# A fused speech-joint forward and backward kernel: pinning the gelu derivative's operations on DVE to their place in the source

## The chip, the cores and the metric

The kernel runs on one core of a Trainium2 chip. The metric is the device time of one execution in microseconds (us). Engines are named as in the profile: PE (TensorE), DVE (VectorE), ACT (ScalarE), POOL (GpSimd) and SP (the queue that issues most loads).

## The reference

The function is a small network and all its gradients. `x` is (2, 16000, 256), `g` is (2, 8, 256), all in bfloat16.

```
h = gelu(conv3(x, w1))[:, ::2]          # 2 x 8000 x 256
f = gelu(conv3(h, w2))[:, ::2]          # 2 x 4000 x 256
fe = f @ w_f;  ge = g @ w_g
j  = tanh(fe[:, :, None] + ge[:, None]) # 2 x 4000 x 8 x 256
out = j @ w_o
# returned: out, and the vjp of grad_out for x, w1, w2, g, w_f, w_g, w_o
```

Backward needs the derivative of both gelus. The gelu is the tanh form, computed as x * sigmoid(A x (1 + K x^2)).

## The kernel before

**Chunks.** Each batch entry has 4000 output rows, cut into 8 chunks: seven of 512 and one of 416, so 16 chunks `n`. For one chunk the forward part is the first convolution (L247, even and odd output rows, `par` 0 and 1), its gelu into `HT`, the second convolution (L280), its gelu into `FT`, and `FE` (L303, L305). The joint part runs over 8 values of `u`, two at a time (`up` 0 to 3): tanh into `JT` (L313), its square `JSQ` (L537), the gradient's product with `w_o` (L543), which DVE turns into `NGZ` (L545, two instructions for each `u`), a running sum of `NGZ` on POOL (L564, tile `ACCN`, the last one `NGFE`), the output matmuls (L641) and their eviction `OUT` (L643, ACT), and the weight gradient `GWO_ps` (L690). In chunk 0 the transposed `JT` that L690 needs is made on PE (L393) and copied by DVE (L395, tile `JR`); in the others a DMA makes it.

**What runs beside what.** `weave` takes the joint units of chunk n as the main line and puts between them, by a ratio, filling units: the forward part of chunk n+1 and the backward part of chunk n-1, which is `GF` (L349, L351, from `NGFE` and `G2`), `GH` (L379, L382, from `GF` and `G1`), the weight gradients (L419, L451, L515, summed on DVE at L332) and the input gradient (L492, evicted by ACT at L495). Chunk 0's forward part runs ahead of the loop, in a prologue.

**The gelu's operations.** `gelu()` issues nothing; it returns two lists. `first` (two on ACT, two on DVE) gives the gelu itself and goes into the queue `later`. `second` gives the derivative (`G1` for the first convolution, `G2` for the second): five DVE operations for each gelu of a chunk, two tensor-scalar and three tensor-tensor operations of 128x1024 bfloat16, and for chunk 0 ten of 128x512. They go into the queue `lazy`, with two small POOL copies of `G1`'s edge column (L259, L263). After each unit of the main line `pump` issues one operation (two while `later` holds some): those of `later` first (their records carry L198), then those of `lazy` (records L200), and these only after `lazy_on` was set at the end of the second convolution:

```
def weave(main, fill, ratio):
    due = 0.0
    for _ in main:
        pump(2 if later else 1)
```

What is left of `lazy` is issued at the end of the chunk. So in the source a chunk's fifteen derivative operations stand behind the second convolution of the same chunk, spread over the units of the last joint pairs.

**What sets the order.** The order on each engine isn't that of the source. The tile framework's scheduler reorders what is independent, and put the derivative operations where their operands are ready, which is earlier than the source has them. An instruction given to `tc.keep_in_program_order` is queued behind the instruction that was traced before it on its engine; it is an order of issue and adds no wait for another engine. Before, only the prologue's warm-up matmuls and the loads `X5` on POOL's queue are pinned.

**Buffers.** The PSUM pool `psp` has 7 banks, shared by all tiles `ps` and `pst`; a matmul that takes a bank waits until the engine that evicts its last content has read it. `JSQ` has 2 buffers, so the square for `u` waits until both `NGZ` of `u-2` are done; `NGZ` has 3 (POOL frees them); the gelu's scratch `g_sq` and `g_s` 3 each; `G1` and `G2` 2.

Of the kernel before, what the change touches and what calls it, by code (L numbers as in the profile page):

```python
# [33 lines left out]
def kernel(  # L34
# [157 lines left out]
    later, lazy = deque(), deque()  # L192
    lazy_on = [False]

    def pump(k):
        for _ in range(k):
            if later:
                later.popleft()()  # L198
            elif lazy and lazy_on[0]:
                lazy.popleft()()  # L200

    def gelu(xb, W, h, gp, off, kts=((0, KT),), spare=False):

# [24 lines left out]
    def conv_units(n):  # L228
# [11 lines left out]
        for par in range(2):  # L240
            xb = gel.tile([P, KT, CW], BF16, name="g_x")
            for mt in range(KT):
                ps = ps_f32()
                k = 0
                for (i, c, sh) in taps[par]:
                    for kt in range(KT):
                        nc.tensor.matmul(ps[:, :W], lhsT=W1[:, i, kt, mt * P:(mt + 1) * P],  # L247
                                         rhs=st["X", c][:, kt, 16 + sh:16 + sh + W], start=(k == 0), stop=(k == 5))
                        k += 1
                nc.scalar.copy(out=xb[:, mt, :W], in_=ps[:, :W])  # L250
                yield
            first, second = gelu(xb, W, HT[:, par], G1[:, par], 2, HALVES if n == 0 else ((0, KT),), n == 0)
            later.extend(first)
            seconds += second
            if n == 0:
                pump(len(first))
# [8 lines left out]
    def conv2_units(n):  # L265
        b, ci, c0, W = geom(n)
        st = S[n]
        HT = st["HT"]
        if n > 0:
            pump(len(later))  # L270
        FT = ftp.tile([P, KT, CW], BF16, name="FT")
        G2 = ftp.tile([P, KT, CW], BF16, name="G2")
        st["FT"], st["G2"] = FT, G2
        xb = gel.tile([P, KT, CW], BF16, name="g_x")
        for mt in range(KT):
            ps = ps_f32()
            k = 0
            for (i, par, off) in ((1, 0, 2), (0, 1, 1), (2, 1, 2)):
                for kt in range(KT):
                    nc.tensor.matmul(ps[:, :W], lhsT=W2[:, i, kt, mt * P:(mt + 1) * P],  # L280
                                     rhs=HT[:, par, kt, off:off + W], start=(k == 0), stop=(k == 5))
                    k += 1
            nc.scalar.copy(out=xb[:, mt, :W], in_=ps[:, :W])
            yield
        first, second = gelu(xb, W, FT, G2, 0, HALVES if n == 0 else ((0, KT),), n == 0)
        if n == 0:
            for f in first:
                f()
        else:
            later.extend(first)  # L290
        lazy.extend(second)
        lazy_on[0] = True

    def fe_units(n):
        b, ci, c0, W = geom(n)
        if n > 0:
            pump(len(later))
        FE = fep.tile([P, KT, CW], FP32, name="FE")
        S[n]["FE"] = FE
        for mt in range(KT):  # L300
            ps = ps_f32()
            for kt in range(KT):
                nc.tensor.matmul(ps[:, :W], lhsT=WF[:, kt, mt * P:(mt + 1) * P], rhs=S[n]["FT"][:, kt, :W],  # L303
                                 start=(kt == 0), stop=(kt == KT - 1))
            nc.scalar.copy(out=FE[:, mt, :W], in_=ps[:, :W])  # L305
            yield
# [595 lines left out]
```

## Time and profile before

| what | value |
|---|---|
| three runs | 857.64, 857.89, 858.03 us; median 857.89 |
| the profiled execution | 858.94 us, its span 857.2 us, so 1.74 us lie outside the span |
| busy in the span | PE 824.1 us (96%), ACT 671.8 (78%), DVE 583.3 (68%), POOL 406.4 (47%) |
| granted TensorE clock | 0.997 of full speed on average |
| L200 records | 15 chunks of 128x1024 or 128x832 operations in 42.1 to 778 us, thirty of 128x512 in 12.9 to 30.5 us |
| the stages | prologue and chunk 0 up to 72.7 us, then about 51.9 us for a full chunk (127.7 to 179.6 us is one) |

A chunk is counted here from the first `GF` eviction (L351) to the next. The chunks are alike from the third on, except where a batch entry ends (384 to 433 us, and the end), so that two stretches stand for all: the first 73 us, and one full chunk.

### The profile page before, as it was taken

The numbers are of one execution on the slowest core, as the hardware profiler recorded it, in microseconds if no ns is written. First come the engines' busy times: TensorE is split into PE (matmuls) and PEld (weight loads), VectorE is DVE, ScalarE is ACT, GpSimd is POOL, SyncE is SP. The second block draws the span as 40 slices with busy tenths as digits, with TensorE's granted clock in tenths as the row PEclk, the third lists the DMA queues.
The fourth block names the chain that finished last, engine by engine and source line by source line (L and its number), as shares of the span: only waits on it lengthen the run. The fifth ranks groups of instructions, "written<-read, shape, count | busy, mean of one in ns | idle before, by whom it ended". The sixth has DMA issues, their size and how long they took to land.

```text
span 857.2 us, 17222 instructions
## 1 busy us (share of the span) xinstructions
PE 824.1 (96%) x6478; PEld 598.7 (70%) x6552; DVE 583.3 (68%) x1190; ACT 671.8 (78%) x1064; POOL 406.4 (47%) x452
## 2 busy tenths in 40 slices
PE   8888999999999999999999999999999999999998
PEld 3455777767668677777767677776776767778876
DVE  4697858658585784859578495875858668495552
ACT  4788897886959869696996959879596886969533
POOL 1255554535535445554553555443553535545650
PEclk9999999999999999999999999999999999999999
DMA  9899999999999999979999999999999999998952
GB/s 189 186 202 219 207 219 221 233 210 216 271 224 226 220 210 267 243 201 231 201 184 215 238 216 238 202 240 257 225 265 210 259 229 191 216 213 199 215 161 90
DMA packets 379280, 185.60 MB, mean 217 GB/s; under 512 B 326786, under 2 KB 362907, under 8 KB 379198
## 3 DMA queue, kind: packets, MB, share of 16 engines
q1 hardware_dynamic: 359550, 115.19, 74.7%
q0 software_dynamic: 19648, 69.32, 26.9%
q8 instruction: 51, 0.84, 0.4%
q14 instruction: 31, 0.25, 0.1%
HBM read 54.43 MB, written 50.34 MB: 122 GB/s over the span
## 4 chain that ended last, share of the span: by engine, by line
ACT 33%; DVE 32%; PE 27%; issue 5%; DMA 2%; POOL 0%; ACTq 0%; DVEq 0%; POOLq 0%
DVE NGZ L545 10%; ACT JT L313 8%; ACT OUT L643 7%; DVE G L200 4%; DVE g_sq L200 4%; ACT JSQ L537 4%; ACT g_sq L198 4%; PE ps L543 4%; DVE GH L382 4%; DVE g_s L198 4%; ACT GX L495 3%; PE ps L515 3%; PE ps L492 3%; PE GWO_ps L690 3%; PE ps L641 3%
## 5 line engine op out<-in xcount | busy, mean ns | idle before, releaser
L564 POOL TENSOR_TENSOR ACCN<-ACCN,NGZ 128x1024 f32<-128x1024 f32 (+1 forms) x80 | 170.7, 2134 | 128.5 <-DVE NGZ L545 126.1
L537 ACT ACTIVATE JSQ<-JT 128x1024 bf16<-128x1024 bf16 (+1 forms) x128 | 133.9, 1049 | 112.4 <-DVE NGZ L545 112.4
L545 DVE SCALAR_TENSOR_TENSOR NGZ<-JSQ,ps 128x512 bf16<-128x512 bf16 (+1 forms) x256 | 163.1, 669 | 77.7 <-PE GWO_ps L690 37.7
L313 ACT ACTIVATE JT<-FE,GE 128x512 bf16<-128x512 f32 (+1 forms) x256 | 171.0, 728 | 0.5
L641 PE MATMUL ps<-WO,JT 128*128 128x256 bf16 x992 | 148.0, 272 | 1.6 <-DVE NGZ L545 0.5
L643 ACT CAST OUT<-ps 128x512 bf16<-128x512 f32 x248 | 145.9, 606 | 2.9 <-PE ps L641 2.8
L690 PE MATMUL GWO_ps<-GO,JR 128*128 128x256 bf16 x992 | 139.9, 273 | 0.0
L543 PE MATMUL ps<-GOT,WOT 128*128 128x512 bf16 (+1 forms) x472 | 134.5, 373 | 3.8 <-DVE JR L395 1.3
L641 PEld LDWEIGHTS <-JT 128*128 128x128 bf16 x992 | 95.5, 98 | 29.5 <-issue 2.2
L198 DVE SCALAR_TENSOR_TENSOR g_s<-g_sq,g_x 128x1024 bf16<-128x1024 bf16 (+1 forms) x45 | 55.9, 1242 | 83.5 <-ACT g_sq L198 83.5
L690 PEld LDWEIGHTS <-JR 128*128 128x128 bf16 x992 | 95.2, 98 | 18.0 <-issue 0.8
L492 PE MATMUL ps<-W1T,GH 128*128 128x256 bf16 (+2 forms) x768 | 104.2, 273 | 0.0
L670 POOL DMA_DIRECT2D out_dram<-OUT x64 | 49.4, 773 | 98.7 <-ACT OUT L643 97.4
L247 PE MATMUL ps<-XC,W 128*128 128x512 bf16 (+1 forms) x370 | 89.7, 377 | 3.3 <-DMA XC<-in_x_dram 2.7
L515 PE MATMUL ps<-rows,X 128*128 128x256 bf16 (+2 forms) x768 | 92.3, 273 | 0.0
L332 DVE TENSOR_TENSOR ACC<-ACC,ps 128x512 f32<-128x512 f32 x84 | 56.1, 682 | 41.5 <-PE ps L515 40.3
L495 ACT CAST GX<-ps 128x512 bf16<-128x512 f32 (+2 forms) x128 | 72.9, 594 | 14.3 <-PE ps L492 11.6
L492 PEld LDWEIGHTS <-GH 128*128 128x128 bf16 (+2 forms) x768 | 75.0, 99 | 12.4 <-issue 1.1
L515 PEld LDWEIGHTS <-X 128*128 128x128 bf16 (+2 forms) x768 | 74.6, 98 | 12.9 <-issue 1.3
L543 PEld LDWEIGHTS <-WOT 128*128 128x128 bf16 x512 | 48.5, 98 | 43.1 <-issue 2.0
L247 PEld LDWEIGHTS <-W 128*128 128x128 bf16 x384 | 37.7, 99 | 41.0 <-issue 4.7
L505 POOL DMA_DIRECT2D out_dram<-GX x60 | 33.7, 561 | 57.7 <-ACT GX L495 51.8
(139 smaller groups left out, 1282.0 us busy)
## 6 DMA issues: line engine op xcount, KB each, us to landing
GO<-in_grad_out_dram SPq DMA_DIRECT2D x56, 512.0 KB, 5.1
out_dram<-OUT POOLq DMA_DIRECT2D x56, 512.0 KB, 5.9
X<-in_x_dram POOLq DMA_DIRECT2D x58, 320.0 KB, 8.6
out_dram<-GX POOLq DMA_DIRECT2D x55, 256.0 KB, 4.2
GO<-in_grad_out_dram SPq DMA_DIRECT2D x8, 384.0 KB, 4.0
out_dram<-OUT POOLq DMA_DIRECT2D x8, 384.0 KB, 4.8
JR<-JT SPq DMA_TRANSPOSE x136, 5.3
GOT<-in_grad_out_dram SPq DMA_TRANSPOSE x128, 4.8
```

The costliest lines, as they stand in the source:

```text
L198: later.popleft()()
L247: nc.tensor.matmul(ps[:, :W], lhsT=W1[:, i, kt, mt * P:(mt + 1) * P], rhs=st["X", c][:, kt, 16 + sh:16 + sh + W], start=(k == 0), stop=(k ...
L313: nc.scalar.activation(out=JT[:, mt, :W], in_=S[n]["FE"][:, mt, :W], func=ACT.Tanh, bias=GE[:, b, mt, u:u + 1], scale=1.0)
L492: nc.tensor.matmul(ps[:Mx, cj * D:(cj + 1) * D], lhsT=GH[:, par, kt, j:j + Mx], rhs=W1T[:, i, kt, :], start=(k == 0), stop=(k == last))
L515: nc.tensor.matmul(ps[:, dt * D:(dt + 1) * D], lhsT=st["X5", o][:M, i + 2 * par, dt * P:(dt + 1) * P], rhs=t[:M, j + 2 * par:j + 2 * par + ...
L537: nc.scalar.activation(out=JSQ[:, :, :W], in_=JT[:, :, :W], func=ACT.Square)
L543: nc.tensor.matmul(ps[:, :W], lhsT=WOT[:, kt, mt * P:(mt + 1) * P], rhs=GOT[:, kt, :W], start=(kt == 0), stop=(kt == KT - 1))
L545: nc.vector.scalar_tensor_tensor(out=NGZ[:, mt, :W], in0=JSQ[:, mt, :W], scalar=1.0, in1=ps[:, :W], op0=ALU.subtract, op1=ALU.mult, accum_ ...
L564: nc.gpsimd.tensor_tensor(out=out, in0=in0, in1=st["NGZ", u][:, :, :W], op=ALU.add)
L641: nc.tensor.matmul(ps[:M, j * V:(j + 1) * V], lhsT=st["JT", u][:, kt, o:o + M], rhs=WO[:, kt, :], start=(kt == 0), stop=(kt == KT - 1))
L643: nc.scalar.copy(out=OUT[:M, k, :], in_=ps[:M, :])
L690: nc.tensor.matmul(GWO_ps[:, dt, :], lhsT=JR[:M, j, dt, k, :], rhs=GO[:M, k, j * V:(j + 1) * V], start=(n_gwo[0] == 0), stop=(n_gwo[0] == ...
```

## The change

One call is wrapped: each operation that `pump` takes from `lazy` is pinned behind the instruction that was traced before it on its engine. The operations and their operands stay as they are.

```
             if later:
                 later.popleft()()
             elif lazy and lazy_on[0]:
-                lazy.popleft()()
+                tc.keep_in_program_order(lazy.popleft()())
```

The built programs differ as follows. On DVE the thirty operations of chunk 0 leave the prologue and stand among chunk 0's `NGZ` and `JR` instructions. The ten `G1` operations of every later chunk, which stood between the last `GH` and the first `NGZ` of pair 2 (mixed with the sums L332), stand behind `FT`: the first five around `NGZ` of `u` = 6, the rest around `u` = 7 and behind it, followed by the five of `G2`. On POOL the two copies L259 and L263 move from behind `GHh` (L386) to behind the third store of `GX` (L505) in the chunk. The order on PE changes in chunk 0 only (where L690, L393, L280 and L543 stand to one another), that on ACT and SP in a few places of the first chunks and where the second batch entry begins.

More of the change, by code (lines that the diff above doesn't have):

```diff
@@ L199, in pump @@
             elif lazy and lazy_on[0]:
-                lazy.popleft()()
+                tc.keep_in_program_order(lazy.popleft()())
     def gelu(xb, W, h, gp, off, kts=((0, KT),), spare=False):
```

## The prediction

> **What bounds the kernel now.** I read the page first, for which engine is full and where it is not.
>
> ```profile
> PE 824.1 (96%) x6478; PEld 598.7 (70%) x6552; DVE 583.3 (68%) x1190; ACT 671.8 (78%) x1064; POOL 406.4 (47%) x452
> PE   8888999999999999999999999999999999999998
> ```
>
> PE is full except at the start, so only waits of PE can be won or added. The table by stretches says what stands beside PE: the prologue, chunk 0, and one full chunk in four parts.
>
> ```profile
> 0.00:32.50 32.50, 25.67 (x143) 12.37 (x146) 19.17 (x59) 17.38 (x29) 5.50 (x14) 1.00 1.01 202
> 32.50:72.70 40.20, 32.00 (x232) 20.80 (x234) 34.90 (x69) 34.41 (x53) 21.23 (x14) 0.96 0.82 180
> 127.70:143.20 15.50, 14.44 (x118) 9.88 (x119) 11.36 (x23) 13.01 (x20) 5.20 (x4) 1.00 1.15 230
> 143.20:155.90 12.70, 12.63 (x103) 9.08 (x102) 12.68 (x24) 5.83 (x9) 7.36 (x9) 1.00 1.15 198
> 155.90:168.00 12.10, 12.05 (x101) 9.69 (x100) 8.29 (x17) 11.74 (x20) 5.67 (x5) 1.00 1.06 272
> 168.00:179.60 11.60, 11.55 (x86) 8.30 (x85) 3.33 (x10) 11.60 (x21) 6.69 (x10) 1.00 1.08 218
> ```
>
> Columns: length, then busy us of PE, PEld, DVE, ACT, POOL. In chunk 0 DVE is nearly full (34.9 of 40.2 us) and PE waits 8 us. In a full chunk DVE is full only from 143.2 to 155.9, where the ten `G1` operations run; ACT then idles, and afterwards is full for 24 us. The timeline of PE has its waits in both places, that of ACT why it idles:
>
> ```profile
> 65.24 0.59 PE L303 MATMUL ps<-FT,WF 128*128 128x512 bf16 x2 [2.97 <-DVE FT L198]
> 71.59 0.59 PE L543 MATMUL ps<-GOT,WOT 128*128 128x512 bf16 x2 [1.28 <-DVE JR L395]
> 137.91 1.03 PE L379 MATMUL ps<-GF,W2T 128*128 128x512 bf16 x4 [0.66 <-DVE GH L382]
> 150.50 1.46 PE L280 MATMUL ps<-HT,W 128*128 128x512 bf16 x6
> 153.55 1.06 ACT L537 ACTIVATE JSQ<-JT 128x1024 bf16<-128x1024 bf16 x1 [6.59 <-DVE NGZ L545]
> ```
>
> Last the timelines of DVE and POOL, for what one moved operation costs:
>
> ```profile
> 46.62 2.23 DVE L198 SCALAR_TENSOR_TENSOR g_s<-g_sq,g_x 128x1024 bf16<-128x1024 bf16 x1
> 58.49 2.56 DVE L200 TENSOR_TENSOR g_sq<-g_sq,HT 128x1024 bf16<-128x1024 bf16 x1
> 143.22 0.42 DVE L200 TENSOR_SCALAR g_sq<-g_sq 128x1024 bf16<-128x1024 bf16 x1
> 143.55 2.69 DVE L200 TENSOR_SCALAR G<-g_s 128x1024 bf16<-128x1024 bf16 x2
> 141.04 4.58 POOL L564 TENSOR_TENSOR ACCN<-ACCN,NGZ 128x1024 f32<-128x1024 f32 x2 [3.49 <-DVE NGZ L545]
> ```
>
> A tensor-scalar operation takes 0.42 us, the pair at 143.55 took 2.69: it stood until POOL's second sum ended at 145.62. That sum in turn began only when the 0.42 us operation before it had ended (two sums, 4.58 us against 2.13 each). So a DVE operation on SBUF alone and a POOL sum exclude each other, and waiting POOL goes first. `NGZ`, `GH`, `JR` and L332 read PSUM and run beside a sum (141.41 and 142.02 do). A derivative operation just behind the first operation that follows an `NGZ` pair thus waits about 2 us.
>
> **Chunk 0.** Thirty 128x512 operations leave the prologue, where they filled idle time from 12.9 to 30.5 us. That gains nothing: PE's next first convolution starts when its `XC` has landed (31.70, waited 2.66), and that load's place in SP's queue hangs on landings, not on DVE. Now the first of them stands behind `NGZ`, which stands behind the `JR` copies at 32.55. I follow DVE in its new order from 32.55, with the spacings of the old timeline: `NGZ` 0.61, `JR` 0.34, 128x512 0.20 (tensor-scalar) or 0.34, 128x1024 0.34 or 0.60 (0.72 where it needs the one before it).
>
> - Work added: 12 x 0.20 + 18 x 0.34 = 8.5 us.
> - Idle used up: DVE idled 4.4 and 0.7 us up to 43 us; in the new order 2.0 us are left: -3.1 us.
> - Waits for POOL: before, five (46.62, 49.77, 58.49, 65.71, 68.93), 6.7 us. After, each of the six sums from `u` = 2 on meets one (at about 46.3, 50.5, 58.5, 62.4, 72.0, 79.3 us): about 11.9 us, +5.2 us.
>
> DVE reaches chunk 1's first `NGZ` at about 83.6 instead of 72.73. PE is held at the same places as before, later: `HT`'s second half ends at 56.1 instead of 51.7 (+4.4), `FT` at 72.05 instead of 65.2 (+6.9), and the `JR` copy whose bank L543 needs at 79.6 instead of 71.5 (+8.1). The first convolution of chunk 1 starts 7.7 us late and waits 0.6 more for a `JR` bank: **+8.2 us**. Later the `NGZ` of chunk 1 have slack again, as ACT sets the next `g_s`. Bounds: +5 if two of the six meetings fail, +11 if all of DVE's delay reaches PE.
>
> A rule bears here. PE gets gaps of up to 2.7 us. In this trace a gap of 2.66 us before 31.70 was followed by a granted clock of 0.85 and 0.81 between 30 and 40 us, 3.4 us at half speed and so 1.7 us of matmul time; the 2.97 us before 65.24 were followed by none. The Trainium skill (TensorE: Matmul & The Clock Gate, "Why this matters for your kernels") advises against PE-idle gaps beyond about 3 us, as a window of idling returns the clock to half rate; by it, gaps of this size are at the edge. The sum takes none; one or two drops are a rival.
>
> **A full chunk.** I keep the old clock of 127.7 to 179.6.
>
> - Gone: from 143.2 on DVE has only the sums and `NGZ`. PE's four small waits for banks (150.50, 152.30, 152.91, 153.51: 0.17 + 0.07 + 0.16 + 0.18) go: 0.58 us. `NGZ` of `u` = 4 ends at 150.7 instead of 153.4, so `JSQ`, `g_x`, `g_s` come 2.3 us sooner or more, and `FT` at 159.6 instead of 161.9; PE needs it at about 161.6, so that gives nothing more.
> - Added behind `FT`: ten operations, no longer in interleaved pairs. From 159.6: tensor-scalar, L332, tensor-scalar, two dependent tensor-tensors; `NGZ` 6a at 162.8 (its matmul sets it), tensor-tensor, 6b to 164.6, tensor-scalar; POOL's sum takes over at 165.0 until 167.2; 7a runs beside it; the next tensor-scalar waits 1.6 us; L332; 7b ends at 168.8 instead of 167.9.
> - What is late next: `JSQ` for the next chunk's `u` = 1 needs 7b. It started at 169.08 with ACT full from 163 on; it could start at 168.3 now, and gets 7b at 168.9. ACT is full from there to the `g_s` that PE's wait at 137.91 hangs on. So a chunk gains 0.2 us where ACT sets its length (eight chunks), not 0.58. The rest (five operations, a second wait, the five of `G2`) ends at 176.3, when the next `NGZ` starts instead of 175.16; its `JSQ` has 0.1 us left.
> - POOL: L259 and L263 leave a place where nothing waited behind them (the sum came at 153.61, for `NGZ`). Now L263 waits for `G1` until 172.9; the copy L370, the last store of `GX` and the `X5` loads queue behind it, and L370 started at 173.36 anyway. SP's swaps in the first chunks move loads by one place: nothing. Both at 0; had they no slack, below 0.5 us a chunk.
>
> Sum: eight chunks x 0.2 = 1.6; the three in which ACT is not yet behind (from 77, 433 and 486 us) give up to 0.58, say 1.3; the 416-row chunk, in which PE waited 0.34 for `FT` at 416.63 and 0.4 for banks, 0.7: **-3.6 us**. Bounds for a full chunk: -0.8 (`7b` meets no sum) to +0.5 (one more spacing of each late operation).
>
> 858.94 + 8.2 - 3.6 = 863.5 for the profiled execution, which lies 1.05 above the median; on the median's side 857.89 + 4.6 = **862.5**.
>
> **Rivals.**
>
> - Forecast, slower by 2 to 10 us: 0.50.
> - The full chunks lose too: if the sum for `u` = 6 gets ahead of the tensor-scalar before 7a, 7b ends 0.7 us later still, and 0.5 us are lost a chunk; if a whole second sum falls ahead of 7b, 1.9. It decides from 7b ending after 169.0. Eleven such chunks: 857.9 + 8.2 + 5.5 = 872, at worst 887. For it: 7b is only 0.2 us from that point. Against: at 143.22 DVE's operation went first. 0.15.
> - One or two clock drops in chunk 0: +1.7 each, 864 to 866. 0.08.
> - Faster: 7b meets no sum, eight chunks gain 0.8, the others as above (8.4 us), and chunk 0 costs 5: 854.5. It decides if 7b ends before 168.1. For it: a quieter DVE in 143 to 156 is the clear effect. Against: `NGZ` 6b always starts a sum ahead of two derivative operations. 0.17.
> - The two cancel, 856.2 to 859.6 (0.2%, about what a measurement of this kernel can tell from no change): 0.10.
> - That the operations don't move is excluded by the built order.
>
> Slower 0.73, same 0.10, faster 0.17. The range 855 to 872 leaves out the worse half of the second and the lower part of the faster case.
>
> **What would show it.** Right: no L200 record before 32 us, waits of about 2 us at L200 or L198 records behind each sum in chunk 0, the first `GF` (L351) at 85 to 88 instead of 76.87, `JSQ`'s 6.59 us wait near 153 down to about 3, no gaps of PE at L280, and chunks of 51.7 us. Wrong: the first `GF` before 82; chunks below 51.3 or above 52.2 us.

## The result, and the profile after

| what | before | after |
|---|---|---|
| median of 22 runs each, taken together | 858.75 us | 861.38 us |
| ratio after to before | | 1.0043 (95% interval 1.0024 to 1.0062), so +3.7 us (+2.1 to +5.3) |
| span of the profiled execution | 857.2 us | 859.6 us |
| granted clock | 0.997 | 0.994 |

The ratio is taken over fast executions alone (one of after's 22 was in a slower state) and isn't the ratio of the two medians, which lie 2.6 us apart. The change makes the kernel slower, by about what was forecast (+4.6 us). Where the time went is read first from the page, then from a table by stretches.

The page of after, first the busy times, then PE's slices:

```profile
PE 821.9 (96%) x6478; PEld 600.1 (70%) x6552; DVE 612.8 (71%) x1190; ACT 679.3 (79%) x1064; POOL 391.1 (45%) x452
PE   8867999999999999999999999999999999999998
```

DVE has the same 1190 instructions as before and is busy 29.5 us longer: time in which operations stand waiting counts as busy. PE's second to fourth slices, 21 to 86 us, read 8, 6, 7 where before had 8, 8, 8. The loss is there; no later slice shows one.

The table by stretches of after (length, then busy us of PE, PEld, DVE, ACT, POOL, the granted clock, the DMA share, GB/s). The second row ends 0.2 us after PE takes up the first convolution of the next chunk (78.90; 72.53 before); the last four rows are the full chunk shown of before, its borders moved with its first `GF`:

```profile
0.00:32.50 32.50, 27.58 (x154) 13.82 (x157) 12.42 (x35) 18.90 (x31) 3.35 (x12) 0.98 1.00 208
32.50:79.10 46.60, 33.56 (x219) 20.93 (x222) 45.41 (x90) 32.99 (x51) 19.48 (x15) 0.90 0.67 150
133.57:149.07 15.50, 14.35 (x116) 9.79 (x117) 10.85 (x22) 13.01 (x20) 5.16 (x4) 1.00 1.12 257
149.07:161.77 12.70, 12.65 (x109) 9.58 (x109) 6.66 (x15) 8.23 (x14) 7.58 (x8) 1.00 1.14 209
161.77:173.87 12.10, 12.05 (x101) 9.69 (x100) 9.68 (x18) 10.47 (x17) 4.05 (x4) 1.00 1.13 278
173.87:185.00 11.13, 11.08 (x82) 7.88 (x81) 10.23 (x21) 11.04 (x20) 6.97 (x11) 1.00 0.97 167
```

In chunk 0 DVE is full (45.4 of 46.6 us) and PE waits 13 us. In the full chunk DVE's full stretch is gone (12.68 became 6.66 us), its load has moved to the last two rows (8.29 and 3.33 became 9.68 and 10.23), and the chunk is shorter.

The timeline of DVE in chunk 0 shows what fills it:

```profile
34.63 0.42 DVE L200 TENSOR_TENSOR rows<-rows,HT 128x512 bf16<-128x512 bf16 x1
34.97 2.22 DVE L200 TENSOR_SCALAR rows<-rows 128x512 bf16<-128x512 bf16 x1
45.47 2.22 DVE L200 TENSOR_SCALAR rows<-rows 128x512 bf16<-128x512 bf16 x1
60.60 2.34 DVE L200 TENSOR_SCALAR g_sq<-g_sq 128x1024 bf16<-128x1024 bf16 x1
69.96 2.35 DVE L200 TENSOR_SCALAR g_sq<-g_sq 128x1024 bf16<-128x1024 bf16 x1
83.42 0.68 DVE L351 SCALAR_TENSOR_TENSOR GF<-G,ps 128x512 bf16<-128x512 bf16 x1
```

A tensor-scalar operation of 0.28 or 0.42 us takes 2.2 or 2.35 wherever it stands second behind an `NGZ` pair. There are seven such meetings, of these and of longer operations, at 34.97, 45.47, 49.36 (`g_s`, 3.14 us), 57.59, 60.60, 69.96 and 77.20 us, and they cost 12.6 us; before, five cost 6.7. The first `GF` comes at 83.42 instead of 76.87.

The timelines of PE and ACT in after, at the places shown of before:

```profile
70.09 0.59 PE L303 MATMUL ps<-FT,WF 128*128 128x512 bf16 x2 [2.79 <-DVE FT L198]
143.87 1.03 PE L379 MATMUL ps<-GF,W2T 128*128 128x512 bf16 x4 [0.74 <-DVE GH L382]
156.74 1.06 ACT L537 ACTIVATE JSQ<-JT 128x1024 bf16<-128x1024 bf16 x1 [3.83 <-DVE NGZ L545]
```

The wait at L379 has grown by 0.08 us, `JSQ`'s wait has shrunk from 6.59 to 3.83, and no wait at L280 is left in the chunk. Taken matmul by matmul, PE's chunk differs from that of before by more than 0.04 us at five places only: L379, and the four small waits (0.17, 0.07, 0.16 and 0.17 us), which are gone.

From here on the executions are cut in three: up to the landing of the `XC` that PE's convolution waits for (31.70 before, 29.94 after), from there to the first `GF` (the stretch of chunk 0), and from the first `GF` to the sixteenth.

| kernel | `XC` lands | stretch of chunk 0 | first to sixteenth `GF` | a middle chunk |
|---|---|---|---|---|
| before | 31.70 | 45.2 | 751.9 | 51.9 |
| before, again | 30.94 | 43.5 | 751.6 | 51.9 |
| after | 29.94 | 53.5 | 747.8 | 51.4 |
| after, again | 31.09 | 54.5 | 746.4 | 51.4 |
| chunk 0 alone pinned | 32.46 | 53.5 | 751.5 | 51.9 |
| pinned from chunk 1 on | 30.67 | 46.7 | 747.7 | 51.4 |
| DVE alone pinned | 31.02 | 53.8 | 753.8 | 51.4 |
| `G1` alone pinned from chunk 1 on | 31.21 | 49.8 | 760.3 | 52.7 |
| pinned, chunk 0's issued early | 31.68 | 47.7 | 746.2 | 51.4 |
| the same, chunk 1's left free | 32.21 | 43.4 | 745.9 | 51.4 |
| cut sums, before | 32.61 | 40.9 | 744.1 | 51.2 |
| cut sums, after | 30.16 | 42.7 | 743.7 | 51.2 |

Of the first pair: -1.8, +8.3 and -4.1, together +2.4 us, as the spans have it (+2.4). The first profile of before has a clock drop at the start of this stretch that costs it 1.7 us (see where the two kernels are profiled again); beside the second, after's loss in chunk 0 is 10.0 us.

### The profile page after: what moved, and what is told of

Read it like the earlier page. It is cut to its first block, busy times and chain, and to the rows that moved or that the text cites. A ratio compares the mean times of both kernels' runs of the same rounds, so it can differ in the third digit from the quotient of the medians.

```text
span 859.6 us, 17235 instructions
## 1 busy us (share of the span) xinstructions
PE 821.9 (96%) x6478; PEld 600.1 (70%) x6552; DVE 612.8 (71%) x1190; ACT 679.3 (79%) x1064; POOL 391.1 (45%) x452
## 4 chain that ended last, share of the span: by engine, by line
PE 52%; ACT 27%; DVE 15%; issue 4%; DMA 1%; ACTq 0%; DVEq 0%
ACT JT L313 9%; PE GWO_ps L690 7%; PE ps L641 7%; PE ps L492 6%; PE ps L543 5%; PE ps L451 5%; PE pst L393 5%; PE ps L515 5%; ACT OUT L643 4%; PE ps L280 4%; ACT JSQ L537 4%; DVE G L200 3%; DVE NGZ L545 3%; PE ps L379 3%; ACT g_sq L198 3%
## 5 line engine op out<-in xcount | busy, mean ns | idle before, releaser
L564 POOL TENSOR_TENSOR ACCN<-ACCN,NGZ 128x1024 f32<-128x1024 f32 (+1 forms) x80 | 167.8, 2098 | 123.8 <-DVE NGZ L545 120.9
L545 DVE SCALAR_TENSOR_TENSOR NGZ<-JSQ,ps 128x512 bf16<-128x512 bf16 (+1 forms) x256 | 165.8, 668 | 26.9 <-PE ps L543 21.6
L543 PE MATMUL ps<-GOT,WOT 128*128 128x512 bf16 (+1 forms) x472 | 135.5, 376 | 5.7 <-DVE JR L395 2.7
L690 PE MATMUL GWO_ps<-GO,JR 128*128 128x256 bf16 x992 | 139.8, 273 | 0.0
L198 DVE SCALAR_TENSOR_TENSOR g_s<-g_sq,g_x 128x1024 bf16<-128x1024 bf16 (+1 forms) x45 | 59.1, 1313 | 82.3 <-ACT g_sq L198 82.3
L690 PEld LDWEIGHTS <-JR 128*128 128x128 bf16 x992 | 95.4, 98 | 18.0 <-issue 1.1
L495 ACT CAST GX<-ps 128x512 bf16<-128x512 f32 (+2 forms) x128 | 74.7, 583 | 23.8 <-PE ps L492 19.1
L543 PEld LDWEIGHTS <-WOT 128*128 128x128 bf16 x512 | 48.9, 98 | 46.2 <-issue 5.8
L332 DVE TENSOR_TENSOR ACC<-ACC,ps 128x512 f32<-128x512 f32 x84 | 57.3, 682 | 28.7 <-PE ps L451 24.1
L505 POOL DMA_DIRECT2D out_dram<-GX x60 | 33.5, 559 | 71.9 <-ACT GX L495 67.9
```

Source lines behind the costliest of these rows:

```text
L543: nc.tensor.matmul(ps[:, :W], lhsT=WOT[:, kt, mt * P:(mt + 1) * P], rhs=GOT[:, kt, :W], start=(kt == 0), stop=(kt == KT - 1))
L545: nc.vector.scalar_tensor_tensor(out=NGZ[:, mt, :W], in0=JSQ[:, mt, :W], scalar=1.0, in1=ps[:, :W], op0=ALU.subtract, op1=ALU.mult, accum_ ...
L564: nc.gpsimd.tensor_tensor(out=out, in0=in0, in1=st["NGZ", u][:, :, :W], op=ALU.add)
L690: nc.tensor.matmul(GWO_ps[:, dt, :], lhsT=JR[:M, j, dt, k, :], rhs=GO[:M, k, j * V:(j + 1) * V], start=(n_gwo[0] == 0), stop=(n_gwo[0] == ...
```

## The experiments

All edits are shown against after; the cut of POOL's sums was made in before as well. Where operations are pinned one by one, `lazy` holds pairs of an operation and a flag (the lines that put the pairs in are left out here):

```
-                tc.keep_in_program_order(lazy.popleft()())
+                f, pin = lazy.popleft(); (tc.keep_in_program_order if pin else id)(f())
```

**Chunk 0 alone, and all but chunk 0.** The flag is `n == 0` in one kernel and `n > 0` in the other, for the derivative operations and POOL's two copies.

> Only chunk 0's thirty derivative operations are pinned, those of later chunks stay with the scheduler. Theory (chunk 0 is the whole loss, the later chunks a separate gain): first GF (L351) at 83 to 85 us against 76.9, later full chunks 51.9 us as before, time 6 to 7 us over before (ratio 1.007 to 1.008). Rival (the later chunks only catch up with what chunk 0 lost, pinned or not): chunks of 51.4 us here too, and the time 2 to 3 us over before.

Measured: ratio 1.0113 (1.0069 to 1.0158) to before, +9.7 us (+5.9 to +13.6), where 6 to 7 were expected; span 865.7. The first `GF` came at 85.95, past the range, as `XC` landed late (32.46). The stretch of chunk 0 is 53.5 us as in after, and later chunks last 51.9 us as before: what chunk 0 loses is never caught up, and the gain of the later chunks belongs to their own pins.

> Pinned from chunk 1 on, chunk 0's thirty operations left to the scheduler, so back in the prologue. Theory: first GF near 76.9 as before, full chunks 51.4 us, no gaps of PE at L280 in a full chunk, time 4 us below before (ratio 0.995); by the recorded sum's own term 3.6 us below. Rival (catching up): chunks 51.9 us, time equal to before. Second rival: the prologue's 1.8 us gain in the profile after belongs to its emptier DVE; then XC lands at 31.7 again here, and at 29.9 in the kernel that pins chunk 0 alone.

Measured: ratio 0.9987 (0.9960 to 1.0014), chunks of 51.4 us. The chunks came as expected; the time is not told from before by its interval, and the stretch of chunk 0 took 46.7 us, 1.5 and 3.2 more than in the two profiles of before. The source issues chunk 1's operations, too, within chunk 0, and those were pinned here. `XC` landed at 30.67 in this kernel and at 32.46 in the one with the empty prologue, so an emptier DVE isn't what lands it early.

**POOL's sums cut to 16 columns of each half, in before and in after.** These kernels leave out most of the running sum.

```
-        acc = st["ACCN"][:, :, :W]
-        in0 = st["NGZ", 0][:, :, :W] if u == 1 else acc
+        w = W if u == U - 1 else 16; acc = st["ACCN"][:, :, :w]
+        in0 = st["NGZ", u if u > 1 else 0][:, :, :w] if u in (1, U - 1) else acc
...
-        nc.gpsimd.tensor_tensor(out=out, in0=in0, in1=st["NGZ", u][:, :, :W], op=ALU.add)
+        nc.gpsimd.tensor_tensor(out=out, in0=in0, in1=st["NGZ", u][:, :, :w], op=ALU.add)
```

> Kernel before with POOL's sums L564 for u = 1 to 6 cut to 16 columns of each half (the one for u = 7 adds NGZ to itself, at full size), so the running sum is left out; the order of instructions on every engine stays. Theory (DVE on SBUF alone waits for the sum): the 46.62, 49.77, 58.49, 65.71 and 143.55 us waits go, first GF 4 to 6 us sooner (71 to 73), chunks 51.4 to 51.7. Rival (those long records have another cause): the records stay at 1.4 to 2.7 us and nothing moves.

> The same cut of POOL's sums in the kernel after; order unchanged on every engine. Theory (of chunk 0's loss some 5 to 6 us is waiting for sums, the rest the 8.5 us of added work less idle time): no L200 or L198 record over 1.5 us between 34 and 76 us except beside the sum for u = 7, first GF 72 to 75, 0 to 3 us behind the cut kernel before instead of 6.5; full chunks 51.2 to 51.5, within 0.3 of the cut kernel before. Rival (the added work alone makes the loss): first GF 5 to 7 us behind the cut kernel before.

Measured: 0.9839 (0.9797 to 0.9880) and 0.9893 (0.9846 to 0.9940) of before's time; the stretches of chunk 0 are 40.9 and 42.7 us. Of the 8.3 us between the first two profiles 1.8 are left, so 6.5 of them were waits for sums. That rules out the rival, 5 to 7 us from the added work alone. (Before and cut before both have the early clock drop, at 33.5 and 33.8 us; without it the loss would be about 1.7 us larger with and without the sums, and the difference would stay.) The first `GF` of the cut kernel before came at 73.55, later than expected because its `XC` landed at 32.61. A middle chunk lasts 51.2 us in both. DVE's timeline in the cut kernel after, four operations that took 2.22, 2.22, 2.34 and 2.27 us in after:

```profile
35.19 0.34 DVE L200 TENSOR_SCALAR rows<-rows 128x512 bf16<-128x512 bf16 x1
44.00 0.34 DVE L200 TENSOR_SCALAR rows<-rows 128x512 bf16<-128x512 bf16 x1
54.05 0.47 DVE L200 TENSOR_SCALAR g_sq<-g_sq 128x1024 bf16<-128x1024 bf16 x1
66.88 2.04 DVE L200 TENSOR_TENSOR g_sq<-g_sq,FT 128x1024 bf16<-128x1024 bf16 x1
```

The first three stand behind cut sums and take their own time. The last stands behind the sum for `u` = 7, which kept its full size, and still waits: the same trace holds its own control.

**Pinned, but issued early.** Chunk 0's thirty operations are issued ahead of the joint loop; everything stays pinned.

```
-    load_jr(0, 0)
+    load_jr(0, 0); pump(len(lazy)); lazy_on[0] = False
```

> Every derivative operation stays pinned, but the source issues chunk 0's thirty right behind the prologue, ahead of the joint loop, instead of one per joint unit. Theory (the place, not the pin, costs the time): DVE has done them by 32 us as before, first GF 76 to 78 (1.5 us around that for a different landing of XC), full chunks 51.4, time 3 to 4 us below before and 6 below after. Rival (pinning itself costs): first GF above 80, time above before.

Measured: 855.89 us against 858.73, ratio 0.9949 (0.9922 to 0.9977): faster than both kernels. The first `GF` at 79.42 lies above the range expected, as the stretch took 47.7 us; 5.8 of the 8.3 us are back. So it is the place that the pin holds them in that costs the time, and not the pin.

**`G1` alone pinned** (flag `n > 0` for `G1` and the copies, `False` for `G2`).

> From chunk 1 on only the ten G1 operations and POOL's two copies are pinned; G2's five and chunk 0's thirty are left to the scheduler, which puts G2's ahead of and among the NGZ of u = 6 and 7, so that five more operations (about 3 us) stand between FT and the second NGZ of u = 7 (7b). Theory, by the recorded step (the square JSQ of the next chunk's u = 1 waits for 7b, and a later 7b is lost in full): 7b 1.5 to 3 us later than in the kernel pinned from chunk 1 on, full chunks 52.5 to 54 us, time 10 to 25 us over before. Rival (ACT has slack there): full chunks 51.4 to 51.9, time as in the kernel pinned from chunk 1 on.

Measured: ratio 1.0107 (1.0073 to 1.0141), +9.2 us, just below the 10 to 25 expected; middle chunks of 52.7 us, 1.3 longer than in after. ACT's timeline shows why:

```profile
174.90 1.06 ACT L537 ACTIVATE JSQ<-JT 128x1024 bf16<-128x1024 bf16 x1 [1.41 <-DVE NGZ L545]
```

This is the `JSQ` for the next chunk's `u` = 1, which in after started without a wait. From the start of the operation that makes `FT`, 7b ended 9.55 us later in after (164.85, 174.40) and 10.86 us later here (163.86, 174.72): 1.3 us, below the 1.5 expected, and all of it is lost in each chunk. The rival that the forecast rated at 0.15 (full chunks lose where 7b comes later) is a real mechanism; in these runs it took G2's operations ahead of 7b to show.

**POOL's copies left free** (flag `True` for DVE's operations, `False` for the two copies).

> As after, but POOL's two copies L259 and L263 are left to the scheduler; only POOL's order differs from after. Theory (recorded step: both at 0): chunks 51.4, first GF 83 to 84 with XC landing as in after, time within 1 us of after. Rival (the copies cost in after): chunks at least 0.2 us shorter, time 2 us or more below after.

Measured: ratio 1.0032 (0.9986 to 1.0077), within the interval of after; middle chunks 51.4 us, the stretch of chunk 0 53.8. The copies' place costs nothing that can be seen. The profiled execution was 7 us longer in one chunk, where PE waited for a transposing load (4.02 us, then 0.80) and the granted clock was 0.50 from 661 to 668 us. No other profile has such a wait, but this program was profiled once, so that it is chance isn't shown. Its PE timeline:

```profile
662.22 0.61 PE L690 MATMUL GWO_ps<-GO,JR 128*128 128x256 bf16 x2 [4.02 <-DMA JR<-JT]
```

**The two kernels profiled again.**

> The kernel before, profiled a second time, for the spread of the prologue between executions. If the landing of XC that starts chunk 0 (31.70 us in the first profile, 29.94 in after) is a matter of chance, it falls anywhere from 29.9 to 32.6 here, and the stretch from it to the first GF stays at 45 to 47 us; if it belongs to the changed program, it is at 31.5 to 32.6 here and at 29.9 to 30.7 in the run that pins DVE alone.

> The kernel after, profiled a second time. If the early landing of XC (29.94 us) in its first profile was chance, it lands anywhere from 30 to 32.6; the stretch from there to the first GF, where DVE never idles, repeats within 0.5 us of 53.5; full chunks 51.42.

Measured: `XC` landed at 30.94 and 31.09 us, so its 29.94 in the first profile of after was chance. The stretches were 43.5 and 54.5 us, both outside what was expected. The timelines of DVE in before and in its second profile say why, at the first `g_s` of the stretch:

```profile
40.83 1.23 DVE L198 SCALAR_TENSOR_TENSOR g_s<-g_sq,g_x 128x1024 bf16<-128x1024 bf16 x1 [4.42 <-ACT g_sq L198]
38.39 1.23 DVE L198 SCALAR_TENSOR_TENSOR g_s<-g_sq,g_x 128x1024 bf16<-128x1024 bf16 x1 [2.75 <-ACT g_sq L198]
```

In the first profile the granted clock was 0.50 from 33.46 to 36.88 us, while PE worked on the convolution that this `g_s` hangs on; in the second it was full there. Counted from the landing of `XC`, `g_s` starts 1.67 us earlier in the second (7.45 instead of 9.13), and the first `GF` 1.67 us earlier too (43.50 instead of 45.17). So the difference of the pair is one clock drop. In the second profile of after the clock was at half from 30.48 to 37.31 us, which spans the landing, and in the first from 31.23 to 34.64; the 1.0 us between the two is there by the first `HT` and no more is added behind it. On the means of the two pairs it costs 54.0 - 44.3 = +9.7 us, and the rest gains 747.1 - 751.7 = -4.6.

**Chunk 0's issued early, chunk 1's left free** (the last edit, and the flag `n != 1`).

> As the kernel with chunk 0's thirty operations issued behind the prologue, and chunk 1's fifteen (which the source issues within chunk 0) left to the scheduler; from chunk 2 on all pinned. Theory (what is left of chunk 0's loss, 2.5 to 3.3 us between XC's landing and the first GF, is chunk 1's operations standing behind NGZ pairs): this stretch back to 43.5 to 45.2 us as in the two profiles of before, chunks 51.4 from chunk 1 on, time 4 to 6 us below before. Rival (that rest is the throttled clock or chance): stretch 46.5 to 48 us, time 2 to 3 us below before.

Measured: 852.75 us against 859.12, ratio 0.9921 (0.9894 to 0.9948), so -6.8 us (-9.1 to -4.5). The stretch is 43.4 us, as in the lower of the two profiles of before, though the clock was at half for the first 5 us of it, and the chunks keep their 51.4. So chunk 1's operations were the rest of the loss. This is the lowest ratio of the kernels with nothing left out (its interval overlaps that of the kernel with chunk 0's issued early), with a late `XC` (32.21) in its profile. Its page has PE's slices:

```profile
PE   8889999999999999999999999999999999999998
```

Where after had 8, 8, 6, 7, chunk 0 is as full as in before, and the fourth slice reaches 9.

## Why the prediction was right, step by step

- **Direction and size.** +4.6 us forecast, +3.7 (2.1 to 5.3) measured. The sum of the two pairs of profiles, chance of `XC` left out, is +9.7 - 4.6 = +5.1. The split was a larger loss and a larger gain than forecast, which nearly cancel; that the total came out so close is partly luck.
- **Prologue, put at 0: right.** The first profile of after seemed to contradict it (-1.8 us), but the order of SP's queue up to and past that load is the same in these kernels, and `XC` landed between 29.9 and 32.6 us in twelve profiles with a full and with an empty DVE alike (29.94 to 32.46 with the prologue empty, 30.67 to 32.61 with it full).
- **Chunk 0, +8.2 us: the mechanism right, the size by luck.** Between the first two profiles it is right to 0.1 us: measured from `XC`'s landing, PE takes up the next convolution at 48.96 instead of 40.83 us (+8.1). But the terms were off. Work added was about 8.5 us as forecast. Waits grew by 5.9 us, not 5.2: seven meetings, since the sum for `u` = 1 meets one too (34.97). Idle used up was 4.0 us, not 3.1 (4.42 and 0.72 before, 1.12 after). DVE reached chunk 1's first `NGZ` 10.0 us later; the forecast has 10.9, where its own three terms add up to 10.6. And the forecast took its spacings, and DVE's idle 4.42 us, from a profile with a clock drop that the changed kernel doesn't pay: beside before's second profile, which has no drop there, the loss is 10.0 us (53.5 - 43.5), and with both second profiles 11.0, the bound of +11.
- **The clock drops, a rival at 0.08.** They came: the granted clock is 0.50 between 32 and 34 us, 0.57 between 48 and 52 and 0.50 between 76 and 78. In this profile they cost next to nothing: DVE has no idle time from 43 to 84 us and sets the end of the stretch, and the kernel with DVE alone pinned, with no drop in its first 19 us, waits the same 1.12 us for the first `HT`. The price of 1.7 us holds where DVE waits for PE: in before's first profile the drop at 33.46 cost 1.67, while in its second the drop at 63.68 cost nothing that shows (6.35 us from L303 to L543's wait in both).
- **Full chunk, -0.2 us: the mechanism right, the size not.** It was -0.48 in each of eight chunks, so -3.8 us instead of -1.6, and 51.42 us instead of 51.7. The mis-sized term is the end of 7b (the two `NGZ` of `u` = 6 and 7 are 6a, 6b, 7a and 7b). Counted from PE's start at L379 (137.91 and 143.87), 6a started at 162.80 and 6b ended at 164.62 on the old clock, both as forecast; POOL's sum ran from 164.86 to 167.03, forecast 165.0 to 167.2; the tensor-scalar operation behind it waited 1.4 us instead of 1.6, and 7b ended at 168.44 instead of 168.8. `JSQ` then started at 168.61 instead of 169.08. PE's four waits gave back 0.57, and its wait at L379 took 0.09 of it.
- **What the four waits were.** With cut sums both orders give chunks of 51.2 us: the order of before then lacks the same four waits, though its ten operations stand where they stood, and PE's matmuls come at the same times in both. So the pin's gain there is that DVE no longer meets a sum ahead of pair 2, not that ten operations left it.
- **The other chunks, -2.0 us together: wrong.** They gave -0.3. The 416-row chunk at the end of the first batch entry gained 0.9 us (forecast 0.7), but the next one took 54.48 us instead of 52.99, and the last stretch but one of the fifteen 0.4 us more than in before. DVE's timeline of after has why:

```profile
438.66 3.59 DVE L198 SCALAR_TENSOR_TENSOR g_s<-g_sq,g_x 128x1024 bf16<-128x1024 bf16 x1 [2.42 <-ACT g_sq L198]
```

A `g_s` of 1.23 us stood 2.4 us, beside a load's issue and a sum on POOL (438.46 to 441.16; which of the two held it first isn't shown), and kept the next `GF` and PE's L379 waiting. How much it costs varies between executions: the same two chunks together took 100.7 and 101.1 us in the profiles of before, and 99.8 to 101.7 in the six with 51.4 us chunks.
- **POOL's copies and SP's swaps at 0.** The copies: right, by the kernel with DVE alone pinned. SP's swaps were not tried by themselves.
- **The tests set beforehand.** No L200 record before 32 us: right, the first is at 32.06. Waits of about 2 us behind each sum: right, 1.3 to 1.9 us. First `GF` at 85 to 88: 83.4 and 85.6, the first below because of its early `XC`. `JSQ`'s wait near 3: 3.83. No gaps of PE at L280: right.

The rule on PE gaps was weighed in the forecast and left out of the sum. The trace differs here from the Trainium skill (TensorE: Matmul & The Clock Gate, "Why this matters for your kernels"), which puts the limit near 3 us of idling. In after, waits of 1.91 us (to 29.94), 2.48 (to 48.34) and 2.23 (to 74.24) were each followed by about 3.4 us at half clock, and the one of 2.79 us at 70.09 was not, directly (the next drop began 5.5 us later).

## What to carry to other kernels

Before pinning an operation to its place in the source, look at what stands around that place on its own engine and on the engine whose operations exclude its own: here a 0.2 us operation cost 2 us behind a sum, and nothing in an idle prologue. Treat the start of a pipeline apart from its steady state; the same pin lost 8 to 11 us in chunk 0, where DVE sets the end, and gained 0.5 us a chunk later, and pinning the later chunks while chunk 0's operations were issued early beat both kernels. A stretch that is cut at a load's landing can be compared between single profiles; from the span alone, 1 to 2 us of landing time pass for an effect. Even then look at the granted clock beside it: one drop at the start of the stretch made 1.67 us.

## What the runs showed of the hardware

- A DVE operation on SBUF alone waits for the whole of a POOL sum of 2.1 us; with the sum cut to 32 columns in all (0.28 to 0.35 us) the wait is 0.05 to 0.06 us. The Trainium skill (SBUF — State Buffer, "Who interferes with whom") describes this as an exclusive lock, held for a whole instruction, and the runs agree. Cutting the sums took the kernel before to 0.984 of its time, 14 us; that bounds what the meetings cost it, as the cut shortens POOL's own work too.
- The same wait of PE at the same matmul (L303, for `FT`: 2.97 us in the first profile of before, 2.96 in the second) was followed by full clock once and by about 3.4 us at half clock once. The rows of the second profile, from 62 us on:

```profile
62.00:64.00 2.00, 1.19 (x14) 0.95 (x14) 2.00 (x6) 1.08 (x2) 1.69 (x1) 0.92 0.83 161
64.00:66.00 2.00, 2.00 (x12) 1.26 (x11) 2.00 (x4) 1.73 (x4) 0.97 (x2) 0.50 0.90 349
66.00:68.00 2.00, 2.00 (x16) 1.55 (x14) 2.00 (x3) 1.73 (x4) 2.00 (x1) 0.73 0.03 10
```

The seventh column is the granted clock. The length of a gap alone does not tell whether a drop follows.
- One drop of 3.4 us at half clock cost 1.67 us where DVE waited for PE's results (before, first profile against second), and nothing that shows where DVE had no idle time.
- The first loads on SP, the same four instructions in every kernel, held its queue for 6.74 to 7.60 us, and the landing that starts chunk 0 spread over 2.7 us in twelve executions.
